# A small expert group in a routed mixture: its ring of weight halves, the weight conversion beside it, and who scales the next group's rows

## The chip, the cores and the metric

The kernel runs on one core of a Trainium2 chip. The metric is the device time of one execution in microseconds (us); lower is better. Times are given as the median of several executions, and the trace is of one further execution under the profiler.

## The reference

Three stages follow one another: attention with a sigmoid in place of the softmax, a top-1 mixture of 8 experts, and a dense feed-forward (FFN) over all 1792 tokens. All data are float32.

```python
attn = 1.0 / (1.0 + np.exp(-(scale * q @ k.T - np.log(S))))   # B=4, H=12, S=448, D=64
x = (attn @ v), rows of 768
...
logits = xn @ en.T / tau                # norms of rows and of expert_emb taken out
expert_idx = np.argmax(logits, axis=1)
gate_w = softmax(logits)[expert_idx]
for e in range(8):                      # w1[e] is 768 x 1024, w2[e] is 1024 x 768
    h = np.maximum(x[mask] @ w1[e], 0.0)
    out[mask] = gate_w[mask, None] * (h @ w2[e])
...
h = x @ w_in                            # 768 x 2048
return (h - np.tanh(h)) @ w_out         # 2048 x 768
```

## The kernel before, in words

Every float32 product is made of three products of rounded halves: high by high, low by high, high by low. A number is split by a cast on ScalarE (ACT), which gives the high half, and by a subtraction on VectorE (DVE), which gives the low one. TensorE (PE) runs the three products.

**Attention** takes 84 slots of scores, hand-ordered on PE (`manual_schedule`). Each slot costs ACT two sigmoids (L275, L276) and DVE one subtraction (L277, tile `al`) that the products with `v` wait for.

**Experts.** Tokens are sorted by expert into groups of 256 rows (`GR`). Two groups are planned early, then six more slots run (`run`, `NST` = 6). A group (`group`) has four column blocks of the first product (`NC1` = 4, tile `pth`, 36 matmuls a block, weights `w1raw`) and three of the second (`NC2` = 3, tile `pty`, 48 matmuls a block, weights `w2raw`). `split` makes the halves of 128 weight columns at a time into `ring`, which has four places (`NRING`), taken in turn by `turns[0]`; so a block uses one pair of places. After the first product of a group, `nxt` gathers the next group's rows by an indirect DMA on GpSimd (POOL), scales them by the gate (`gate_rows`, ACT, L807), transposes them on PE and splits them (`columns`: ACT L840, DVE L841, tiles `wi`, `xl`). A gathered group waits in `xg`; `wi0` holds the high half of its columns, so there is one such tile.

**The small slot.** One expert has a rest of at most 128 rows. It is done right after the first planned slot (`NFEW` = 1) by `prep_few` and `few`, with the operands exchanged: 128 rows stand still and 256 weight columns stream, 18 matmuls a block of the first product and 24 of the second. Weights are split by halves of the depth (`both(c, 0)` and `both(c, 1)`): block 0 goes to two tiles of its own (`few_h`, `few_l`), the others to pairs of the ring, listed in `s["parts"]`. Its results come out with rows standing and have to be turned (`turn`, two transposes through PSUM tile `xt`, of which there are two): `hidden` turns a block of the middle layer and splits it, `out` turns a block of the result. The PSUM tiles `xt` are shared with `columns`. Three chains (`A`, `V`, `T`, class `Line`) keep the small slot's own instructions on ACT, DVE and PE in the order in which they are written; all else is placed by a scheduler that works out times and priorities when the program is built. Each engine then runs its list in order.

**Conversion.** The FFN weights are split once into DRAM: 32 units (`conv_unit`), each with a load and a store on the queue of SyncE (SP) and seven instructions: ACT L1147 and L1158, DVE L1149, L1151, L1153, L1155, L1160 (tiles `ca`, `cr`). `NEARLY` units run in attention, `CPG` units are handed to each expert group until eight (`NFFN`) are left, and the last eight run in the FFN (`CPF`). In the experts they are put in at a low priority (`LATER`), behind the scaling of the next group's rows (`issue_after(self.xg_act.ins)`).

## Time and profile before

| what | us |
|---|---|
| median of 3 executions (1026.67 to 1028.25) | 1027.68 |
| the profiled execution, its own time | 1028.11 |
| its span, first to last instruction | 1026.4 |
| PE busy, share of the span | 993.7 (97%) |
| DVE busy | 786.8 (77%) |
| ACT busy | 554.3 (54%) |
| POOL busy | 218.5 (21%) |

Attention runs to about 223 us, the experts from there to about 544, the FFN from there to the end. In the profile a stretch is read by the number of PE instructions in it: matmuls of 256 columns follow each other about every 0.118 us when nothing is missing, so 8 us hold about 69 of them. A row's bracket, where there is one, gives the idle time ahead of it and what ended that.

### The profile page before, as it was taken

What the parts mean: (1) busy time and instruction counts of PE and PEld (TensorE: products, weight loads), DVE (VectorE), ACT (ScalarE), POOL (GpSimd) and SP (SyncE); (2) the same over time, 40 slices, a digit from 0 to 9 for tenths busy, and PEclk for the clock granted to TensorE, in tenths of its full rate; (3) what the DMA queues carried; (4) which work ended last, traced back from release to release, by engine and by line L of the source; (5) the groups of instructions that cost most, each with busy time, mean ns of one, the idle gap of its engine ahead of it and who ended that gap; (6) DMA issues with size and microseconds to landing.
All of it is one profiled execution on the core that took longest, in us unless ns stands there. A gap on an engine that the chain in (4) does not pass through costs nothing.

```text
span 1026.4 us, 16537 instructions
## 1 busy us (share of the span) xinstructions
PE 993.7 (97%) x6318; PEld 923.1 (90%) x6318; DVE 786.8 (77%) x1043; ACT 554.3 (54%) x698; POOL 218.5 (21%) x312
## 2 busy tenths in 40 slices
PE   8999999999998789999999999999999999999997
PEld 6877878789998789999999899999999999999997
DVE  6687777769977878989854888998897667766774
ACT  7788887876575767676643434344343332333230
POOL 8667667645800100100000000000001200000002
PEclk9999999999999989999999999999999999999999
DMA  6533434369568985965814555345524531233212
GB/s 174 138 89 116 119 85 123 113 213 369 208 216 278 358 294 191 332 218 193 270 64 152 193 175 185 144 170 185 197 111 154 200 112 65 102 123 118 98 62 108
DMA packets 83446, 174.87 MB, mean 170 GB/s; under 512 B 7623, under 2 KB 62942, under 8 KB 83358
## 3 DMA queue, kind: packets, MB, share of 16 engines
q1 hardware_dynamic: 79438, 155.56, 44.9%
q0 software_dynamic: 3760, 17.95, 4.9%
q8 instruction: 52, 0.85, 0.3%
q14 instruction: 36, 0.29, 0.1%
q10 hardware_dynamic: 160, 0.21, 0.1%
HBM read 156.28 MB, written 36.30 MB: 188 GB/s over the span
## 4 chain that ended last, share of the span: by engine, by line
issue 57%; PE 26%; ACT 6%; DVE 5%; POOL 3%; DMA 2%; SPq 0%; POOLq 0%; ACTq 0%; DVEq 0%
PE pth L902 8%; PE pty L902 7%; PE pav L291 5%; PE pq L268 4%; ACT ah L275 2%; ACT pq L276 2%; POOL out_dram L546 2%; PE pr L316 1%; DVE al L277 1%; DMA xg<-x_tok,gidx 1%; DMA kq<-in_k_dram 1%; ACT sq L333 1%; DVE ring L991 1%; PE xt L834 1%; PE pty L991 1%
## 5 line engine op out<-in xcount | busy, mean ns | idle before, releaser
L1306 PE MATMUL o<-wo,gh 128*128 128x384 f32 x896 | 240.4, 335 | 0.7 <-DVE acc L1319 0.7
L1255 PE MATMUL z<-yh,wi 128*128 128x512 f32 (+1 forms) x768 | 220.0, 365 | 0.4 <-PEq L1122 0.4
L1306 PEld LDWEIGHTS o<-wo,gh 128*128 128x128 f32 x896 | 163.0, 188 | 2.2 <-DVE acc L1319 1.0
L1255 PEld LDWEIGHTS z<-yh,wi 128*128 128x128 f32 x768 | 141.6, 188 | 15.7 <-issue 0.6
L1306 PE MATMUL o<-wo,gl 128*128 128x384 f32 x448 | 150.0, 335 | 0.5 <-DVE gl L1280 0.5
L902 PE MATMUL pth<-wi,ring 128*128 128x256 f32 x768 | 140.2, 282 | 1.2 <-DVE ring L893 0.6
L1255 PE MATMUL z<-yl,wi 128*128 128x384 f32 (+1 forms) x384 | 138.3, 364 | 0.0
L902 PE MATMUL pty<-hh,ring 128*128 128x256 f32 x736 | 136.9, 284 | 1.3 <-ACT ring L892 1.2
L546 POOL DMA_INDIRECT out_dram<-acc,toki x14 | 16.7, 1193 | 570.3 <-DVE acc L1319 569.1
L277 DVE TENSOR_TENSOR al<-pq,ah 128x896 fp32r<-128x896 f32 x84 | 91.3, 1088 | 43.5 <-ACT pq L276 43.3
L902 PEld LDWEIGHTS pth<-wi,ring 128*128 128x128 f32 x768 | 119.0, 189 | 2.4 <-DVE ring L893 0.8
L902 PEld LDWEIGHTS pty<-hh,ring 128*128 128x128 f32 x736 | 116.0, 191 | 1.8 <-ACT ring L892 1.5
L1319 DVE TENSOR_TENSOR acc<-o,acc 128x768 f32<-128x768 f32 x97 | 92.4, 953 | 31.8 <-PE o L1306 31.6
L902 PE MATMUL pth<-xl,ring 128*128 128x256 f32 x384 | 108.1, 282 | 0.0
L1279 ACT CAST gh<-r 128x896 fp32r<-128x896 f32 x32 | 30.1, 941 | 140.8 <-DVE r L1277 79.3
L902 PE MATMUL pty<-hl,ring 128*128 128x256 f32 x368 | 104.2, 284 | 0.3 <-DVE hl L920 0.3
L275 ACT ACTIVATE ah<-pq,bias_s 128x896 fp32r<-128x896 f32 x84 | 85.5, 1018 | 34.9 <-PE pq L268 34.2
L1263 ACT ACTIVATE t<-z 128x896 f32<-128x896 f32 x32 | 29.4, 920 | 107.2 <-PE z L1255 66.4
L1306 PEld LDWEIGHTS o<-wo,gl 128*128 128x128 f32 x448 | 84.1, 188 | 2.2 <-DVE gl L1280 0.8
L276 ACT ACTIVATE pq<-pq,bias_s 128x896 f32<-128x896 f32 x84 | 83.0, 988 | 0.0
L1255 PEld LDWEIGHTS z<-yl,wi 128*128 128x128 f32 x384 | 72.1, 188 | 7.4
L893 DVE TENSOR_TENSOR ring<-w1raw,ring 128x768 fp32r<-128x768 f32 x64 | 60.5, 953 | 23.5 <-ACT ring L892 23.2
(317 smaller groups left out, 1946.1 us busy)
## 6 DMA issues: line engine op xcount, KB each, us to landing
w1raw<-in_moe_w_dram SPq DMA_DIRECT2D x36, 768.0 KB
w2raw<-in_moe_w_dram SPq DMA_DIRECT2D x27, 1024.0 KB
wi<-dwi SPq DMA_DIRECT2D x32, 768.0 KB
wo<-dwo SPq DMA_DIRECT2D x32, 768.0 KB
cr<-in_moe_w_in_dram SPq DMA_DIRECT2D x16, 768.0 KB
dwi<-cr SPq DMA_DIRECT2D x16, 768.0 KB
cr<-in_moe_w_out_dram SPq DMA_DIRECT2D x16, 768.0 KB
dwo<-cr SPq DMA_DIRECT2D x16, 768.0 KB
```

What stands on the lines that cost most here:

```text
L268: nc.tensor.matmul(pq[:, x, :S], w[kt][p, c : c + P], w[qt][p, KW:], start=(m == 0), stop=(m == 2))
L275: nc.scalar.activation(hi, pv, AF.Sigmoid, **sc)
L276: self.last_sig = nc.scalar.activation(pv, pv, AF.Sigmoid, **sc)
L277: nc.vector.tensor_tensor(lo, pv, f32(hi), ALU.subtract)
L291: nc.tensor.matmul(pav[:, :S], vo(vv), aa[:, x], start=(b0 and m == 0), stop=(e and m == 2))
L546: i = self.nc.gpsimd.indirect_dma_start(**kw)
L893: self.last_split = nc.vector.tensor_tensor(wl, cols, f32(wh), ALU.subtract)
L902: self.last_mm = nc.tensor.matmul(pt[:, u], a[:, kk], b[:, kk], start=(n == 0), stop=(n == 3 * K - 1))
L1255: nc.tensor.matmul(z[:, G0[g] : G0[g] + GS[g]], wi[:, a, j * P : (j + 1) * P], yhl[half][g][b][:, j], start=(left[g] == 3 * NJ), stop=(lef ...
L1279: nc.scalar.copy(gv, r)
L1306: nc.tensor.matmul(o[:, w, :NW], a[:, u, i * P : (i + 1) * P], wo[:, b, w * NW : (w + 1) * NW], start=(n == 0), stop=(n == 3 * CH - 1),)
L1319: nc.vector.tensor_tensor(acc[i], ov, acc[i], ALU.add)
```

## The change

Six edits.

1. Conversion: `NEARLY` goes from 1 to 3 units in attention, and `CPG` from 6 for each group to the list 3, 4, 0, 4, 4, 3, 3, 0; the third entry is the group after which the small slot comes.
2. Ring: the first pair of the small slot is now the one after the pairs that the group's own second product takes (`NC2` = 3 further), so the order in which pairs are taken goes on without a pair being taken twice in a row.
3. Rows: behind the small slot's group the next rows are scaled by POOL (`pool=True`, `tensor_scalar`) instead of ACT. ACT's next `gate_rows` comes after the small slot's last ACT instruction (`issue_after(self.last_few)`).
4. PE: the small slot's matmuls come after the last matmul of its group (`T.last`).
5. Splits: the second half of a block's split is written after the turn of the block ahead (`hidden`), not together with the first half.
6. `nxt` is called one half block earlier.

```diff
-NEARLY, NFFN = 1, 8
+NEARLY, NFFN = 3, 8
-CPG, CPF = 6, 2
+CPG, CPF = (3, 4, 0, 4, 4, 3, 3, 0), 2
...
     def gate_rows(self, s, h):
-        self.xg_act = self.nc.scalar.activation(x[:, h, :DM], x[:, h, :DM], AF.Copy, scale=x[:, h, DM + 1 : DM + 2])
+        with self.tc.issue_after(self.last_few) if self.last_few is not None else ExitStack():
+            self.xg_act = self.nc.scalar.activation(x[:, h, :DM], x[:, h, :DM], AF.Copy, scale=x[:, h, DM + 1 : DM + 2])
...
+            if pool:
+                x = s["x"][:, h]
+                self.nc.gpsimd.tensor_scalar(x[:, : self.DM], x[:, : self.DM], x[:, self.DM + 1 : self.DM + 2], None, ALU.mult)
+            else:
+                self.gate_rows(s, h)
...
-                    for _ in range(CPG):
+                    for _ in range(conv.pop(0)):
...
-            k = turns[0] % NRING // 2
+            k = (turns[0] // 2 + NC2) % 2
...
         def few(s, nxt):
+            T.last = self.last_mm.ins
...
                     hidden(c - 1)
+                if c > 1:
+                    both(c + 1, 1)
                 product(c, pt, s["xt"], 1)
                 keep(c, pt, nc.scalar.activation, AF.Relu)
                 if c in (1, 2):
                     both(c + 2, 0)
-                    both(c + 2, 1)
...
                     both(NC1 + 1, 1)
+                    nxt()
...
                     both(NC1 + 2, 1)
-                    nxt()
             T.last = None
             out(NC2 - 1)
+            self.last_few = A.last
...
-                nxt = (lambda: prep(slots[i + 1], n)) if i + 1 < len(slots) else None
+                nxt = (lambda: prep(slots[i + 1], n, here)) if i + 1 < len(slots) else None
```

Three places show what this does to the lists of the engines.

PE where the first product of the small slot's group ends. `pth<-wi,ring` and `pty` of L902 (L908 in the new numbering) are the group's, all of L991 are the small slot's. Before:

```order
1359 L902 MATMUL pth<-wi_124,ring 128x256
1360 L991 MATMUL pth<-few_h,wi_124 128x256
1361 L962 MATMUL xt<-ident,xg 128x128 x2
1362 L964 MATMUL xt<-ident,xg 1x128
1363 L991 MATMUL pth<-few_h,wi_124 128x256
1364 L991 MATMUL pth<-few_l,wi_124 128x256
1365 L991 MATMUL pth<-few_h,wi_124 128x256 x2
...
1369 L902 MATMUL pty<-hh,ring 128x256
1370 L902 MATMUL pty<-hl,ring 128x256
```

After:

```order
1359 L908 MATMUL pth<-wi_124,ring 128x256
1360 L968 MATMUL xt<-ident,xg 128x128 x2
1361 L970 MATMUL xt<-ident,xg 1x128
1362 L908 MATMUL pty<-hh,ring 128x256
1363 L908 MATMUL pty<-hl,ring 128x256
1364 L908 MATMUL pty<-hh,ring 128x256
1365 L908 MATMUL pty<-hl,ring 128x256
```

Thirteen of the 18 matmuls of the small slot's first block stood between the group's two products; now they stand behind the group's last one.

ACT at the end of the group, with the first splits into the ring for the small slot (`ring<-w1raw_141`), before:

```order
304 L941 COPY yT_2705<-pty 128x2x256
305 L807 ACTIVATE xg<-xg 128x768 x2
306 L941 ISA
307 L941 COPY yT_2706<-pty 128x2x256
308 L991 CAST ring<-w1raw_141 128x3x2x128
309 L1147 ACTIVATE ca<-cr 128x768
310 L991 CAST ring<-w1raw_141 128x3x2x128
```

After:

```order
307 L947 COPY yT_2727<-pty 128x2x256
308 L997 CAST ring<-w1raw_141 128x3x2x128 x2
309 L947 ISA
310 L947 COPY yT_2728<-pty 128x2x256
311 L997 CAST ring<-w1raw_142 128x3x2x128 x2
```

The split of block 1 moved ahead of the group's second result, the scaling of rows (L807) and the conversion (L1147) left the place.

ACT at the start of the group that follows the small slot (`hh<-pth` is its first result block), after:

```order
339 L898 CAST ring<-w1raw_142 128x768
340 L997 ISA
341 L997 COPY yT_last<-xt 128x2x128
342 L809 ACTIVATE xg<-xg 128x768 x2
343 L1158 ACTIVATE ca<-cr 128x768 x2
344 L898 CAST ring<-w1raw_142 128x768
345 L925 ACTIVATE hh<-pth 128x512
```

Two scalings of rows and the first instructions of two units now stand ahead of `hh`; before, one scaling, one split and the end of a unit stood there:

```order
347 L991 COPY yT_last<-xt 128x2x128
348 L807 ACTIVATE xg<-xg 128x768
349 L892 CAST ring<-w1raw_142 128x768
350 L1158 CAST cr<-ca 128x768
351 L892 CAST ring<-w1raw_142 128x768
352 L919 ACTIVATE hh<-pth 128x512
```

What moved there is the second scaling, which came behind `hh`, and the units' first instructions.

## Rows read from the trace of the kernel before

**Rows 1.** Busy time by stretch: length, PE, PEld, DVE, ACT, POOL (instructions), clock, DMA.

```profile
224.00:312.00 88.00, 87.30 (x734) 86.51 (x735) 76.01 (x152) 58.12 (x84) 40.18 (x40) 1.00 0.81 276
312.00:384.00 72.00, 60.27 (x456) 56.72 (x455) 56.32 (x74) 49.27 (x73) 7.11 (x6) 0.93 0.89 310
384.00:544.00 160.00, 160.00 (x1348) 159.41 (x1347) 127.39 (x154) 100.01 (x132) 6.45 (x4) 1.00 0.61 203
...
360.00:368.00 8.00, 6.19 (x29) 5.70 (x30) 5.35 (x8) 2.74 (x5) 1.89 (x2) 0.51 1.03 381
```

**Rows 2.** Who waited for whom, PE, 312 to 384 us: total, times, longest.

```profile
PE xt L825 <- DVE xl L841: 2.6, 1, 2.6
PE xt L834 <- DVE xl L841: 2.0, 1, 2.0
```

**Rows 3.** Timeline of PE ahead of the second product: start, us, line, tiles, count.

```profile
314.47 0.28 PE L902 MATMUL pth<-wi,ring 128*128 128x256 f32 x1
315.55 0.39 PE L991 MATMUL pth<-few_h,wi 128*128 128x256 f32 x1 [0.81 <-ACT few_h L994]
...
319.08 0.28 PE L991 MATMUL pth<-few_h,wi 128*128 128x256 f32 x1
320.61 0.39 PE L902 MATMUL pty<-hh,ring 128*128 128x256 f32 x1 [1.25 <-ACT ring L892]
```

**Rows 4.** Timeline of PE in the small slot and behind it.

```profile
347.97 0.28 PE L991 MATMUL pty<-ring,hh 128*128 128x256 f32 x1
...
358.06 1.12 PE L834 MATMUL xt<-ident,xg 128*128 128x128 f32 x4 [2.02 <-DVE xl L841]
361.80 0.58 PE L825 MATMUL xt<-ident,xg 128*1 128x128 f32 x2 [2.62 <-DVE xl L841]
...
366.50 0.63 PE L991 MATMUL pty<-ring,hh 128*128 128x256 f32 x2
366.93 0.41 PE L991 MATMUL pty<-ring,hl 128*128 128x256 f32 x1
...
380.07 0.36 PE L902 MATMUL pth<-wi,ring 128*128 128x256 f32 x1 [0.30 <-DVE hl L920]
```

**Rows 5.** Groups by line, DVE, 337 to 364 us: count | busy, mean | idle.

```profile
L991 DVE TENSOR_TENSOR ring<-w2raw,ring 128x1024 fp32r<-128x1024 f32 x6 | 7.2, 1223 | 0.0
L991 DVE TENSOR_TENSOR ring<-w1raw,ring 128x768 fp32r<-128x768 f32 x6 | 5.6, 952 | 8.4 <-ACT ring L991 8.3
L1160 DVE TENSOR_TENSOR cr<-ca,cr 128x768 fp32r<-128x768 f32 x3 | 2.9, 954 | 0.0
...
L841 DVE TENSOR_TENSOR xl<-xt,wi 128x512 fp32r<-128x512 f32 x3 | 2.0, 686 | 0.0
...
L1149 DVE TENSOR_SCALAR ca<-ca 128x768 f32<-128x768 f32 x3 | 1.7, 553 | 0.0
```

**Rows 6.** Groups by line, ACT, 337 to 364 us.

```profile
L991 ACT CAST ring<-w1raw 128x768 fp32r<-128x768 f32 x6 | 4.7, 832 | 3.3 <-PE pty L902 3.3
L1147 ACT ACTIVATE ca<-cr 128x768 f32<-128x768 f32 x3 | 2.8, 919 | 0.6 <-DMA cr<-in_moe_w_in_dram 0.6
...
L807 ACT ACTIVATE xg<-xg 128x768 f32<-128x768 f32 x2 | 1.9, 934 | 0.0
```

**Rows 7.** Attention, 57 to 77 us: PE's waits, and one conversion step on DVE.

```profile
PE pq L268 <- DVE al L277: 0.9, 2, 0.5
...
59.94 1.25 DVE L1151 TENSOR_SCALAR ca<-ca 128x768 int32<-128x768 int32 x1
```

**Rows 8.** Groups by line, POOL, whole span: nearest operations to a scaling of rows.

```profile
L229 POOL TENSOR_TENSOR w2l<-kq,w2h 128x512 fp32r<-128x512 f32 x8 | 10.3, 1287 | 0.0
...
L464 POOL TENSOR_SCALAR lg<-u,itau 112x32 f32<-112x32 f32 x4 | 4.8, 1204 | 13.1 <-DVE u L326 13.1
```

**Rows 9.** An earlier rest of PE in attention, and the stretch behind it.

```profile
19.31 0.47 PE L268 MATMUL pq<-w2h 64*128 64x448 f32 x2 [1.32 <-DVE al L277]
...
20.00:22.00 2.00, 2.00 (x8) 1.47 (x5) 1.12 (x2) 2.00 (x3) 2.00 (x2) 0.50 0.75 229
```

More of the change, by code (lines that the diff above doesn't have):

```diff
@@ L765, in experts_early @@
     def experts_early(self, cx):
+        self.last_few = None
         self.pp = self.pool("plan", 1, cx)
@@ L806, in gate_rows, with gather_rows @@
         DM, x = self.DM, s["x"]
-        self.xg_act = self.nc.scalar.activation(x[:, h, :DM], x[:, h, :DM], AF.Copy, scale=x[:, h, DM + 1 : DM + 2])
-    def gather_rows(self, pl, slot):
+        with self.tc.issue_after(self.last_few) if self.last_few is not None else ExitStack():
+            self.xg_act = self.nc.scalar.activation(x[:, h, :DM], x[:, h, :DM], AF.Copy, scale=x[:, h, DM + 1 : DM + 2])
+    def gather_rows(self, pl, slot, pool=False):
         s = self.group_tiles(pl, slot)
@@ L813, in gather_rows @@
         for h in range(2):
-            self.gate_rows(s, h)
+            if pool:
[3 more added lines that the diff above has]
+                self.gate_rows(s, h)
         return s
@@ L946, in experts, with prep @@
         pst = lambda: ps.tile([P, 2, GR], F32, tag="x", name="xt")
-        def prep(slot, s):
-            s.update(self.gather_rows(pl, slot))
+        def prep(slot, s, pool=False):
+            s.update(self.gather_rows(pl, slot, pool))
             self.columns(s, pst)
@@ L1111, in second @@
             self.columns(self.s1, pst)
-        group(self.s0, self.e0, None, slice(0, GR), NWE, second, True, last_route)
+        conv = list(CPG)
+        group(self.s0, self.e0, None, slice(0, GR), NWE, second, conv, last_route)
         e, new = (self.reg(nc.sync, self.pl1[x], 0, n) for x, n in (("e", E - 1), ("new", 1)))
         oa = self.reg(nc.scalar, self.pl1["off"], 0, NT - 1)
-        group(self.s1, e, new, ds(oa, GR), 0, lambda: prep(0, s), True)
-        run(list(range(NST)), s, True, False)
+        group(self.s1, e, new, ds(oa, GR), 0, lambda: prep(0, s), conv)
+        run(list(range(NST)), s, conv, False)
         first = lambda: nc.sync.dma_start(f32(self.wi0).rearrange("p a b -> p (a b)"), self.win_s[0].rearrange("p a b -> p (a b)"))
         first()
+        self.last_few = None
         if NG > NST:
@@ L1126, in experts @@
                 prep(NST, s)
-                run(list(range(NST, NG)), s, False, True)
+                run(list(range(NST, NG)), s, None, True)
                 first()
```

## The prediction

> **What bounds the kernel now.** I read the busy times by stretch first. TensorE is busy through nearly all of the 1026.4 us, so the time falls only where PE stands still or runs slowly. From 384 to 544 us PE does 1348 matmuls in 160 us, 0.119 us each, with no gap; from 312 to 384 us it does 456 in 72 us [rows 1]. At 0.119 these are 54.3 us of work, so about 18 us are lost, in the small slot and its surroundings. The reader should see that this is the only large hole.
>
> The waits name three losses. First, ahead of the group's second product PE waits for the small slot's operands and then 1.25 us for a ring split, so the second product gets going at 320.61 [rows 3]. Second, in the small slot it waits 2.0 and 2.6 us for low halves of the next rows, both put down to DVE [rows 2, 4]. That engine holds 6 + 6 ring splits and three conversion units there [rows 5]: a unit is three steps of two operands at 0.954 and two of one at 0.553, 3.97 us, so three take 11.9 of 26.4 us in which DVE has no break. Third, the clock: behind those rests it is granted at 0.51 [rows 1], half of 2.4 GHz, and matmuls follow each other every 0.213 us (two and one more from 366.50 to 366.93, [rows 4]). A mean of 0.93 over 72 us is 0.07 x 72 / 0.5 = 10 us at 1.2 GHz, in which each us loses (0.213 - 0.119) / 0.213 = 0.44 us. Before 352 us there is no place for them, so the shorter rests of [rows 3] left the clock alone.
>
> **The change part by part.** Times of the replay are estimates from durations of before laid on the new order.
>
> *Filler moved.* Of the small slot's first block, 13 matmuls stood in the rest before the second product. They go behind it: 13 x 0.119 = +1.5 us there. The rest itself stays: its first products wait for ACT's splits of the group's own weights, which no edit moves, so 320.61 holds.
>
> *Second product and small slot.* The group's second product has 144 matmuls, 4 of them done; 140 more end at 337.2, the 18 of block 0 at 339.4. The ring in step lets the split of block 1 begin while the group's last product runs; with splits at 0.83 on ACT and 0.95 on DVE [rows 6, 5] they are then ready, and blocks 1 to 3 run at PE's pace: 54 x 0.119 = 6.4, to about 346 with the turns. In before PE began the second product of the small slot at 347.97 [rows 4]; so 1.5 late has become about 1.5 early. With 11.9 us of conversion gone, DVE waits for PE here and no longer PE for DVE.
>
> *Who is late next.* The last but one block. Its splits of `w2raw` can begin only when the turns are through, about 350; then DVE has four of these at 1.22, three low halves of the next rows at 0.69 and a short step, estimated at 0.4: 7.3 us [rows 5], of which the turn that ends the block's first half waits for all. So PE reaches the turn at about 357.3, where before it stood at 362.39 [rows 4], after a rest of some 3 us in an almost empty stretch of 4.5. Behind it stand 36 matmuls and the turns, 4.9 us at full clock: 362.2. In before the same ran at half clock to 369.4. Gain here: 5.0 + 2.2 = 7.2.
>
> *The group that follows.* PE is ready for its third block after two blocks of 36 and the transposes, 9.5 us later at 371.7; in before this block starts at 380.07, waiting for `hl` [rows 4]. But ACT now holds two scalings of rows (2 x 0.93) and two conversion starts (2 x 0.92) [rows 6] ahead of the first `hh`, behind a copy that waits for the small slot's last turn, which PE does 34 matmuls into this group, at 366. Copy to 366.5, scalings to 368.4, starts to 370.2, a split to 371.0, `hh` to 371.6; on DVE the units' one-operand steps and a split stand ahead of `hl`, which ends at 373.7. So PE waits 2.0 and the gain shrinks to 380.07 - 373.7 = 6.4. Two later waits of the same kind (conversion ahead of a low split and of a further `hl`), at one or half a DVE step of 0.95 each, cost 1.4. **Experts: -5.0**, bounds -7.2 (no queue late) and -3.5 (each twice as long). With 384 to 544 full, nothing behind it can give more back.
>
> *Clock.* With the filler gone, from 314.6 to 320.6 PE does three transposes and four matmuls, where it did 13 matmuls more [rows 3]. In attention a rest ending at 19.31 was followed by a granted clock of 0.50 [rows 9]; the rests of [rows 3] were not. Between none and eight us at half clock (0 to 3.6), I take **+1.5**. The rest before the turn at 357.3 is shorter than the 2.0 + 2.6 that made the clock fall in before: 0 to 2.3, I take **+0.8**.
>
> The Trainium skill, "TensorE: Matmul & The Clock Gate", section "What's actually happening", says that the throttled state is the default and activity releases it. By this a stretch that loses its filler would lose clock too, as [rows 9] shows and [rows 3] does not; by it alone the sum would be higher by the 2.1 us left open here.
>
> *Attention.* Two more units there. Where the one of before ran, PE waited 0.9 us for `al` [rows 7], with none in the neighbouring stretches. Two give **+1.8**; bounds 0 (they fall where DVE has room) and 3.0 (a step took 1.25 us there against 0.553 in the experts [rows 7, 5]).
>
> *Fewer units in other groups.* 21 in place of 23, but in stretches without waits: nothing. The small slot's group hands out none.
>
> *POOL.* The rows of the next group are needed at about 346, and gathered near 320. No scaling on POOL is in the trace. Its nearest rows are 1.20 us for 32 columns with a scalar for each partition and 1.29 for 512 columns of two operands [rows 8]; between 1.2 and 3.1 us each for 768, so two end by 330 at the latest. Zero; if a queue of POOL held them 15 us longer, it would count. ACT is relieved of 1.9 us in the rest, worth little, as PE waits there for splits ahead of it.
>
> A step of DVE took twice its usual time in attention beside POOL work [rows 7, 5]. The Trainium skill, "SBUF — State Buffer", section "SBUF: two separate sides", says that GpSimd and VectorE share a pair of ports that one instruction holds whole. By it DVE's low splits could stand behind each scaling, at most 2 x 3.1 us; the replay has over 3 us of room there, so it would leave up to 3 more.
>
> *Splits interleaved, `nxt` earlier.* Within the order replayed above.
>
> *Sum.* -5.0 + 1.5 + 0.8 + 1.8 = -0.9, on the profiled execution's 1028.11, which is 0.4 above the median of 1027.68. The forecast on the median is **1026.9**, -0.8. A difference of 0.2%, 2.06 us, is about what a measurement of this kernel can tell; the forecast lies within it.
>
> **The rivals.**
>
> *Faster: clock stays up.* The rests of [rows 3] did not cost clock and the new one is broken up by small work. Then both clock terms are zero: -5.0 + 1.8 = -3.2, about 1024.4; with the following group's queue on time -7.2 + 1.8 = -5.4, 1022.3. I put this case at 1023.4. For it: only one rest in 312 to 352 would be new. Against: the stretch 314.6 to 320.6 is nearly empty.
>
> *Slower: clock falls in both rests and stays down through dense work.* Place: from 320.61 on, the second product, and again from 357.3 on. Price 0.44 us per us. At the bounds, 3.6 + 2.3 against -5.0 + 1.8: +2.7, 1030.4. It decides from 3.2 us of clock loss on for any loss at all, and from 5.3 us, twelve us of dense work at 0.213, for over 0.2%. For it: in before 10 us went at half clock after one such rest [rows 1, 4]. Against: it needs both.
>
> *The change does not do what it says.* If the small slot's splits were early enough anyway, since its first block now starts a group later than the filler did, the ring step would move nothing, and conversion in the next groups takes back what it left: 1027.7.
>
> **How the numbers follow.** Forecast 0.40; faster rival 0.35; slower rival 0.19; no effect 0.06. The range reaches to both rivals, 1022.5 to 1030.6; the forecast's own is 1025.6 to 1029.7. Faster by over 0.2% 0.35, within 0.46, slower 0.19.
>
> **What would show it right or wrong.** In the trace of after: no conversion step on DVE from 337 to 362; no wait for low halves of rows of 2 us in the small slot; 456 matmuls of this stretch done before 384, and the third block of the next group starting near 373.7 in place of 380.07, plus what the clock took. The granted clock behind 320 and behind 357 tells the two clock terms apart: 1.00 in both is the faster rival, 0.5 for eight us behind 320 the slower. `hh` of the next group behind two scalings and two conversion starts, and waits of PE for it, show the queue term. The end of attention moving from 223 to about 225 shows the attention term. The prediction is wrong if the second product starts later than 320.61, if POOL's rows come after 346, or if a full stretch behind 384 gets gaps.

## The result

The changed kernel is slower. Its median is 1038.01 us (four runs, 1037.03 to 1041.91), against 1027.18 for the kernel before; the ratio is 1.0114, with a 95% interval of 1.0084 to 1.0145. That is 10.8 us more, outside the range of 1022.5 to 1030.6, and on the side to which the prediction gave 0.19. The profiled execution has a span of 1037.0 us, where that of before has 1026.4.

The first step is to cut the span at three places that can be read from the timeline of PE: the first matmul of the experts (`pth`), the last matmul of the small slot, and the first matmul of the FFN (`z`). The lengths between them, in us, worked out from the starts and ends of those rows:

| kernel | attention, to the first `pth` | from there to the small slot's end | from there to the FFN | FFN |
|---|---|---|---|---|
| before | 223.1 | 146.7 | 179.3 | 477.3 |
| after | 230.3 | 138.8 | 190.2 | 477.7 |
| difference | +7.2 | -7.9 | +10.9 | +0.4 |

So the stretch for which the change was written did become shorter, by about what was forecast. It was lost twice: ahead of it in attention and behind it in the groups that follow.

PE by stretch in the kernel after (length, then busy time and instructions of PE, PEld, DVE, ACT, POOL, then granted clock and DMA; a granted clock of 1.00 is 2.4 GHz, 0.50 is 1.2 GHz, and what lies between is a mix of the two). The row of 312 to 384 answers to that of [rows 1]; the row of 24 to 216 is attention without its two ends. The last row is that of the kernel before for attention:

```profile
24.00:216.00 192.00, 182.32 (x1072) 147.83 (x1071) 145.78 (x245) 156.00 (x195) 126.16 (x197) 0.99 0.42 129
312.00:384.00 72.00, 63.42 (x506) 61.15 (x505) 51.60 (x66) 45.95 (x69) 14.20 (x8) 0.95 0.80 264
408.00:424.00 16.00, 12.66 (x101) 11.84 (x100) 10.68 (x14) 10.01 (x14) 0.00 (x0) 1.00 0.52 173
448.00:464.00 16.00, 13.34 (x96) 12.73 (x95) 7.66 (x11) 7.78 (x11) 0.00 (x0) 0.89 0.54 193
...
24.00:216.00 192.00, 185.97 (x1106) 151.81 (x1104) 141.38 (x241) 158.03 (x197) 127.66 (x202) 1.00 0.40 119
```

In 312 to 384 us PE now does 506 instructions in place of 456, although everything there comes 7.2 us later. In exchange two stretches that were full before have holes: at 0.119 us each, 16 us hold some 135 matmuls, and here stand 101 and 96.

**Where attention loses.** Two places of the timeline, VectorE and then PE (start, length, engine, line, tiles; in brackets the idle time ahead and what ended it):

```profile
133.02 1.09 DVE L277 TENSOR_TENSOR al<-pq,ah 128x896 fp32r<-128x896 f32 x1 [1.00 <-ACT pq L276]
134.03 1.61 DVE L1160 TENSOR_SCALAR ca<-ca 128x768 f32<-128x768 f32 x1
135.67 0.70 DVE L1162 TENSOR_SCALAR ca<-ca 128x768 int32<-128x768 int32 x1
136.41 1.09 DVE L1164 SCALAR_TENSOR_TENSOR ca<-cr,ca 128x768 int32<-128x768 int32 x1
137.53 0.96 DVE L1166 SCALAR_TENSOR_TENSOR ca<-cr,ca 128x768 int32<-128x768 int32 x1
138.41 1.08 DVE L277 TENSOR_TENSOR al<-pq,ah 128x896 fp32r<-128x896 f32 x1
...
139.55 0.47 PE L268 MATMUL pq<-w2h 128*128 128x448 f32 x1 [2.65 <-DVE al L277]
...
140.60 0.57 PE L268 MATMUL pq<-w2h,w2l 128*128 128x448 f32 x1
```

Four steps of the third unit stand in a clump ahead of the subtraction `al` that PE needs: 4.4 us. PE rests for 2.65 us, and from about 140 us its matmuls are further apart; the granted clock of 136 to 144 us is 0.79. The second unit is cheaper. It shows as a step of 1.26 us on VectorE at 112.33, beside which POOL takes 3.11 us for a pair of products that take 2.40 elsewhere, and PE waits 1.39 us for POOL at 115.74.

**Where the groups behind lose.** POOL, ACT, DVE and PE around the first of the two holes; the last two rows are the gathers at these two places in the kernel before:

```profile
397.61 8.64 POOL L800 DMA_INDIRECT xg<-x_tok,gidx  x1 [0.30 <-issue]
...
411.60 0.93 ACT L809 ACTIVATE xg<-xg 128x768 f32<-128x768 f32 x1 [7.30 <-DMA xg<-x_tok,gidx]
412.44 0.81 ACT L898 CAST ring<-w1raw 128x768 fp32r<-128x768 f32 x1
...
413.28 0.96 DVE L899 TENSOR_TENSOR ring<-w1raw,ring 128x768 fp32r<-128x768 f32 x1 [7.26 <-ACT ring L898]
...
413.31 0.38 PE L908 MATMUL pth<-wi,ring 128*128 128x256 f32 x1 [1.51 <-ACT ring L898]
414.30 0.50 PE L908 MATMUL pth<-wi,ring 128*128 128x256 f32 x2 [0.49 <-DVE ring L899]
417.77 0.50 PE L908 MATMUL pth<-wi,ring 128*128 128x256 f32 x2 [1.07 <-DVE ring L899]
...
395.98 0.94 POOL L799 DMA_INDIRECT xg<-x_tok,gidx  x1 [0.30 <-issue]
430.96 3.61 POOL L799 DMA_INDIRECT xg<-x_tok,gidx  x1 [0.30 <-DVE ca L1153]
```

This is read from top to bottom. POOL needs 8.64 us to issue a gather that takes 0.94 in the kernel before. The rows land about 5 us later. ACT has come to the scaling of these rows and waits for them 7.30 us, since it does its list in order; the weight splits behind it start late, then VectorE's, then PE's matmuls. At 437 us the same happens again: 10.28 us of POOL, 7.28 of ACT, 1.98 of PE, and behind that the clock at 0.79.

The loss can be put to groups by counting their matmuls (144 of the second product in each). From the small slot's end, the five groups take 37.9, 35.5, 35.8, 36.3 and 33.4 us in the kernel before, and 40.0, 39.3, 41.6, 35.8 and 33.2 here. So 2.1 us are lost in the group next to the small slot, where PE waits for `hl`, and 3.8 and 5.8 in the two groups whose rows come late.

### The profile page after: what moved, and what is told of

Same layout as the page of the kernel before. It is cut to its first block, busy times and chain, and to the rows that moved or that the text cites. A ratio compares the mean times of both kernels' runs of the same rounds, so it can differ in the third digit from the quotient of the medians.

```text
span 1037.0 us, 16535 instructions
## 1 busy us (share of the span) xinstructions
PE 998.4 (96%) x6318; PEld 926.5 (89%) x6318; DVE 786.7 (76%) x1043; ACT 552.5 (53%) x696; POOL 235.8 (23%) x314
## 4 chain that ended last, share of the span: by engine, by line
issue 54%; DMA 2%; POOL 2%; PE 1%; ACT 0%; DVE 0%; POOLq 0%
DMA xg<-x_tok,gidx 2%; POOL out_dram L546 2%; PE pth L908 1%; PE pty L908 0%; ACT ring L898 0%; POOLq L1448 0%; ACT cr L1169 0%; POOL xg L800 0%; DVE hl L926 0%; DVE ring L899 0%; DVE cr L1171 0%; ACT wi L846 0%; ACT yT_last L947 0%; POOLq L546 0%; POOLq L1133 0%
## 5 line engine op out<-in xcount | busy, mean ns | idle before, releaser
L908 PE MATMUL pth<-wi,ring 128*128 128x256 f32 x768 | 142.9, 285 | 8.6 <-ACT ring L898 3.5
L908 PE MATMUL pty<-hh,ring 128*128 128x256 f32 x736 | 138.3, 286 | 3.6 <-ACT ring L898 3.6
L908 PEld LDWEIGHTS pth<-wi,ring 128*128 128x128 f32 x768 | 119.9, 190 | 11.0 <-ACT ring L898 4.1
L908 PEld LDWEIGHTS pty<-hh,ring 128*128 128x128 f32 x736 | 117.3, 194 | 4.3 <-ACT ring L898 4.2
L908 PE MATMUL pth<-xl,ring 128*128 128x256 f32 x384 | 108.6, 283 | 0.0
L908 PE MATMUL pty<-hl,ring 128*128 128x256 f32 x368 | 105.0, 286 | 0.0
```

The costliest lines, as they stand in the source:

```text
L908: self.last_mm = nc.tensor.matmul(pt[:, u], a[:, kk], b[:, kk], start=(n == 0), stop=(n == 3 * K - 1))
```

## The experiments

The theory after the result has two parts. **A:** the two added units cost attention the 7 us. **B:** the scaling that waits on ACT for a late gather costs the groups the 11 us; behind it stands **C**, that the gather is late because VectorE runs without a pause beside it. The rival to A is that any new placement costs that much; the rival to B is that VectorE is too full there in itself, or that the weights arrive late.

### One conversion unit in attention: e1_near1

```diff
-NEARLY, NFFN = 3, 8
-CPG, CPF = (3, 4, 0, 4, 4, 3, 3, 0), 2
+NEARLY, NFFN = 1, 8
+CPG, CPF = (3, 4, 0, 4, 4, 3, 3, 2), 2
```

> The changed kernel with one conversion unit in attention instead of three; the two others go to the last expert group, which has none. Theory A (the two units cost attention about 8.4 us: four conversion steps of 4.4 us on VectorE ahead of one subtraction al at 138.4 us, PE waits 2.65 us and its clock falls behind it): attention ends near 223 us again, the granted clock is 1.00 from 136 to 144, time 1038.0 - 8.4 = about 1029.6. Rival (the loss in attention is not the units' but comes with any new placement, as the routing steps on VectorE and GpSimd move too): attention still ends 5 us or more late, time above 1035.

Measured: 1025.82 us, ratio to before 0.9979 (0.9969 to 0.9990). It is 12.2 us faster than the changed kernel, more than expected. Attention ends at 223.7 us, 6.6 less, and there are 1109 instructions of PE from 24 to 216 us: A holds. The other half of the gain was not expected: from the small slot's end to the FFN it takes 183.2 us in place of 190.2, though the two groups still get four units each. The gathers show why. The first takes 1.26 us, the second 6.56, and ACT waits 3.9 us for rows in these groups, in place of 14.6. With attention 7 us shorter, the scheduler laid the steps on VectorE in another order, and the gather met another stretch of them. The amount of conversion does not tell the two apart: in the 73 us behind the small slot VectorE spends 30.6 us on it here and 27.7 in the changed kernel.

### The third unit alone: e9_after_near2

```diff
-NEARLY, NFFN = 3, 8
-CPG, CPF = (3, 4, 0, 4, 4, 3, 3, 0), 2
+NEARLY, NFFN = 2, 8
+CPG, CPF = (3, 4, 0, 4, 4, 3, 3, 1), 2
```

> The changed kernel with two conversion units in attention instead of three, the third in the last group. Theory A in detail (each unit's steps come in a clump of four on VectorE ahead of a subtraction; the second unit's clump at 98 to 104 us costs about 2 us, the third's at 134 to 138 costs about 4.5, its own 2.65 us rest and the clock behind it): the rest at 136 to 139 and the fall of the clock there are gone, 1038.0 - 4.5 = about 1033.5. Rival (a fixed price for each unit wherever it falls, 8.4 / 2 = 4.2 each, of which the second pays as much): the loss from 96 to 120 us is as large as the one removed; both rivals give about the same time, but the matmuls of PE by 120 us and by 150 us tell them apart: theory A has 13 to 20 fewer than the kernel before at 120 and no more at 150, the rival 25 fewer by 120.

Measured: 1028.96 us, ratio 1.0010 (0.9996 to 1.0024). From 24 to 216 us PE does 1099 instructions, against 1072 with three units, 1109 with one and 1115 with none (e12_e7_near0). At 192 / 1106 = 0.174 us each, the third unit costs 27 x 0.174 = 4.7 us, the second 1.7 and the first 1.0. Profiles with the same attention code differ by about 1 us of this: 1104 to 1110 instructions in the nine with one unit, 1072 to 1078 in the three with three units. So the third unit's price is shown, at 3.7 to 4.7 us, and the others' only roughly. The rest at 136 us and the fall of the clock are gone (1.00 granted). Counted from 24 us, it lacks 13 instructions of the kernel before by 120 us, 9 by 128 and 8 by 152, which is theory A's picture. The price is not the same for each unit; it hangs on where its clump of steps falls. Here too the groups gain beside that (182.4 us from the small slot's end to the FFN), with gathers of 1.24 and 6.55 us.

### Rows scaled by GpSimd in every group: e2_pool_all

```diff
-                self.nc.gpsimd.tensor_scalar(...)
+                self.xg_act = self.nc.gpsimd.tensor_scalar(...)
...
-                nxt = (lambda: prep(slots[i + 1], n, here)) ...
+                nxt = (lambda: prep(slots[i + 1], n, not first)) ...
```

> The changed kernel with the rows of every following group scaled by GpSimd, not only those behind the small slot's group. In the changed kernel ScalarE's scaling waits twice 7.3 us for the second gather, and the weight splits behind it in ScalarE's list come late. Theory B (that wait in ScalarE's order is what stops PE at 411 and 454): no weight split waits there, PE's waits of 1.5 and 2.0 us and the clock's fall are gone, though the gathers still take 8 to 10 us of GpSimd; time 1038.0 - 10 = about 1028. Rival (VectorE itself is too full there, or the weights arrive late): PE's waits stay, time above 1035. Second rival: the scaled rows come so late that the transposes in the second product wait for them, which PE then shows at another place, 1033 to 1040.

Measured: 1025.83 us, ratio 0.9985 (0.9972 to 0.9998), 12.2 us faster than the changed kernel. From the small slot's end to the FFN it takes 178.3 us, 11.9 less, and PE has no wait there up to the first matmul of the FFN. By group it is 3.1 us less in the first, where no scalings stand ahead of `hh` any more, 3.7 in the second and 5.8 in the third. Attention, whose code is the same, is 2.2 us shorter in this profile. A gather of 9.55 us is still in the trace, with scalings of 8.36 us for two behind it on POOL, and nobody waits for them; but it stands one group earlier. The first line of the edit hangs the conversion on GpSimd's scaling, its order is new, and the gathers of the two groups that lost are short here (1.28 to 1.66 us). So this run takes away ACT's wait and the late rows at once. The two are told apart by e8_e6_ring below: there the gathers of these same groups take 7.88 and 6.38 us, GpSimd scales, and the groups take 35.5 and 35.8 us, as in this run. B holds: it was ACT's place in the chain, not the lateness of the rows. That VectorE was too full there is excluded too, as it has more conversion behind the small slot here (29.9 us in 73) than in the changed kernel (27.7).

### No conversion in the two groups: e3_units_late

```diff
-CPG, CPF = (3, 4, 0, 4, 4, 3, 3, 0), 2
+CPG, CPF = (3, 4, 0, 0, 0, 5, 5, 4), 2
```

> The changed kernel with no conversion in the two groups behind the small slot; their eight units go to the three groups after these (5, 5 and 4). Theory C (a gather on GpSimd ends only when VectorE comes to a pause, and the conversion closes the pauses): the gathers of the two groups take 1 to 2 us instead of 8.6 and 10.3, ScalarE's scaling does not wait there, PE has no gap from 384 to 460; where conversion now is dense, later gathers take 5 us or more, and one or two losses of 5 us stand there instead: time 1028 to 1038. Rival (the gather is long because of its own data or queue at that place): the same two gathers stay at 8 to 10 us without conversion beside them.

Measured: 1036.26 us, ratio 1.0084 (1.0062 to 1.0106). The same gathers are short: 0.94 and 1.40 us in the first group, 1.00 and 1.70 in the second. ACT waits 2.0 us for rows in place of 14.6. That is for C and against a gather that is long by itself. My guess on where the units would then hurt was wrong: no gather is left by then, but the FFN waits for the last units. PE waits 4.9 us for `yh` ahead of the FFN's first matmul and later 2.4 for a load of `wi`, and from that first matmul on the FFN takes 482.8 us in place of 477.7. The five groups themselves are done in 179.5 us, against 189.8 in the changed kernel and 178.9 before.

### The kernel before with the list alone: e4_before_nosmall and e5_before_list

The first takes from the kernel before only what the small slot's group hands out, the second gives it the list of the changed kernel with one unit in attention.

```diff
-CPG, CPF = 6, 2
+CPG, CPF = (6, 6, 0, 6, 5, 0, 0, 0), 2     (first)
+CPG, CPF = (3, 4, 0, 4, 4, 3, 3, 2), 2     (second)
...
+                    for _ in range(conv.pop(0)):
```

> The kernel before with one edit alone: the small slot's group hands out no conversion (6, 6, 0, 6, 5 units by group instead of 6, 6, 6, 5). Theory D (the conversion on VectorE is what the small slot waited for, so most of the 7.8 us that the changed kernel gains there come from this edit): the rests of 2.0 and 2.6 us and the clock's fall behind them go, gain of 5 to 8 us in the small slot; if the two groups behind it then lose as in the changed kernel, 2 to 10 us are given back, as read from their gathers. Rival (the ring order or the interleaved splits make the gain): the small slot keeps its waits of 2 us and more, time within 2 us of before or above.

Measured: 1027.26 us, ratio 0.9998 (0.9986 to 1.0011). Theory D cannot be told by this run: three units still stand on VectorE from 337 to 364 us, the small slot keeps its rests of 2.0 and 3.1 us, and the clock falls to 0.57 granted from 360 to 368. What the small slot meets are units handed out by the groups ahead, which have not been done by then.

> The kernel before with the conversion list 3, 4, 0, 4, 4, 3, 3, 2 alone (one unit in attention as before, and none of the other edits). In the run with 6, 6, 0 the small slot still held three units on VectorE, left over from the groups ahead, and kept its waits; here only seven are handed out ahead of it. Theory D, mended (the units handed out earlier than the small slot, not its own entry, decide; without any unit there the small slot loses its rests): no conversion step on VectorE from 337 to 364, the waits of 2.0 and 2.6 us and the half clock behind them gone, small slot 5 to 8 us shorter; of this the two groups behind may give back 3 to 10 by long gathers. Rival (ring in step and interleaved splits are needed for it): a rest of 2 us or more and a fallen clock stay in the small slot.

Measured: 1027.87 us, ratio 0.9996 (0.9982 to 1.0010). Now less than half as much conversion stands on VectorE in that stretch (4.8 us by its rows, 11.9 before), and the small slot ends 5.3 us earlier (141.4 us behind the start of the experts, 146.7 before). So the list alone gives two thirds of the 7.9 us. The expectation holds only in part: the rest of 2.0 us is down to 0.3, but one of 2.2 us stays where 2.6 stood, and the clock still falls behind it, for a shorter time (0.66 granted from 358 to 360 us, 0.50 to 362). All of the gain is given back: 186.1 us from there to the FFN in place of 179.3, all in the first group (44.7 us in place of 37.9). The profiled execution took 1031.23 us, 3.4 above the median, so the loss is read from it with care. Here is the reason, POOL, ACT, VectorE and PE behind the small slot in this run:

```profile
361.81 12.62 POOL L799 DMA_INDIRECT xg<-x_tok,gidx  x1 [0.30 <-PE pty L991]
...
377.86 0.94 ACT L807 ACTIVATE xg<-xg 128x768 f32<-128x768 f32 x1 [5.65 <-DMA xg<-x_tok,gidx]
...
372.68 0.94 DVE L1154 SCALAR_TENSOR_TENSOR ca<-cr,ca 128x768 int32<-128x768 int32 x1
373.55 0.67 DVE L920 SCALAR_TENSOR_TENSOR hl<-pth,hh 128x512 fp32r<-128x512 f32 x1
...
379.57 0.58 PE L902 MATMUL pth<-wi,ring 128*128 128x256 f32 x1 [3.68 <-ACT ring L892]
```

The gather ends at 374.43, 0.88 us behind the start of the subtraction `hl`, which has an operand from PSUM (`pth`). From the gather's issue to it, 11.7 us, stand fifteen instructions of VectorE with all operands in SBUF, without a pause.

### Both repairs: e6_near1_pool_all

The edits of e1_near1 and e2_pool_all together.

> The changed kernel with both repairs: one conversion unit in attention (the other two to the last group) and the rows of every following group scaled by GpSimd. If the two losses are separate, as theory A and B have it, their repairs add up: 12.2 and 12.2 us taken off one after the other, less what the first alone already saved of the second (its ScalarE waits were 3.9 instead of 14.6 us): 1019 to 1021. Rival (both repairs act by the same thing, the place of the conversion units in the two groups): no better than either alone, 1025.

Measured: 1020.93 us, ratio 0.9928 (0.9909 to 0.9946): as expected, 17.1 us below the changed kernel. The two repairs overlap by 7.3 us, since the first alone had already shortened the gathers and with them this stage by 7.0 us. Attention ends at 224.7, the small slot takes 139.0, the groups behind it 178.1.

### The fourth edit undone: e7_e6_filler

```diff
-            T.last = self.last_mm.ins
```

> The run before with the fourth edit undone: the small slot's matmuls may again stand ahead of the group's second product. Theory E (the edit empties the rest of PE ahead of the second product, and the clock falls behind it: 27 matmuls too few from 312 to 328 in the first run of this study, and 0.79 granted in the changed kernel): the filler comes back, granted clock 1.00 there, 2 to 3.5 us faster than the run before. Rival (the small slot's block needs the splits of the group's place, and its early start only moves waits): within 1 us, or slower by the two splits that then stand ahead.

Measured: 1016.8 us, ratio 0.9897 (0.9880 to 0.9914), 4.1 us better than the run before it. PE by stretch ahead of the group's second product, in e6_near1_pool_all and then here:

```profile
312.00:320.00 8.00, 4.95 (x36) 4.15 (x34) 7.96 (x12) 6.88 (x11) 1.68 (x2) 0.89 0.63 246
320.00:328.00 8.00, 6.54 (x41) 6.54 (x42) 7.34 (x9) 3.40 (x4) 6.25 (x3) 0.68 0.83 244
...
312.00:320.00 8.00, 5.26 (x36) 4.22 (x36) 7.96 (x12) 7.57 (x12) 2.48 (x2) 1.00 0.58 212
320.00:328.00 8.00, 8.00 (x68) 8.00 (x69) 7.86 (x8) 3.33 (x4) 5.97 (x2) 1.00 0.83 252
```

The second product runs at full clock here. It does so in the kernel before and in e5_before_list as well; in e4_before_nosmall and in the three runs that follow, which keep the filler too, the clock falls at this place (0.70 to 0.77 granted from 320 to 328 us). So the filler does not hold the clock every time. The small slot's stage takes 139.0 us in e6_near1_pool_all, 137.1 to 137.8 in the three runs that keep the filler and lose the clock, and 135.3 here. That puts some 1.5 us on the filler, which is also what 13 matmuls take by count, and some 2 on the clock; it is one profile each, so the shares are an estimate.

### The second edit undone: e8_e6_ring

```diff
-            k = (turns[0] // 2 + NC2) % 2
+            k = turns[0] % NRING // 2
```

> The run with both repairs with the second edit undone: the small slot's first pair of the ring is again the one used last by its group. Theory F (the pair taken twice in a row makes the first split wait for the group's last product): ScalarE's split for block 1 waits again for PE's last pty, PE waits 0.7 us and more for the ring in blocks 1 and 2 of the small slot, and the parity seen by the following group moves too; 1 to 3 us slower. Rival (the first block of 18 matmuls now hides the split): within 0.7 us.

Measured: 1026.22 us, ratio 0.9986 (0.9974 to 0.9999), 5.3 us slower than e6_near1_pool_all. The size was more than expected and the place another. In the small slot's blocks 1 to 3 PE waits for no split at all, so the rival is right there. The small slot ends 2.0 us later, with a wait of 1.5 us for a copy that stands behind two splits on ACT. The other 4.7 us lie behind it: two conversion casts, another conversion start and two splits now stand ahead of the next group's `hh`, PE waits 2.4 us for `hl` at 375.83, and the clock falls (0.79 from 376 to 384 us); that group takes 41.6 us in place of 36.9. How much of that is the ring and how much the scheduler's new order for the conversion, this run does not tell.

The groups after it lose nothing, though two of their gathers are long. POOL, and then all engines by stretch (length, PE, PEld, DVE, ACT, POOL, clock, DMA):

```profile
393.69 7.88 POOL L800 DMA_INDIRECT xg<-x_tok,gidx  x1 [0.30 <-issue]
431.89 6.38 POOL L800 DMA_INDIRECT xg<-x_tok,gidx  x1 [0.30 <-issue]
...
400.00:416.00 16.00, 16.00 (x137) 16.00 (x137) 13.00 (x15) 9.51 (x13) 7.04 (x3) 1.00 0.96 318
432.00:448.00 16.00, 16.00 (x137) 16.00 (x136) 14.64 (x16) 9.17 (x13) 11.12 (x3) 1.00 0.93 315
```

These are the gathers behind which the changed kernel lost 3.8 and 5.8 us. With the scaling on GpSimd the rows are as late (the second half is scaled 47 and 85 us behind the small slot's end, against 43 and 86 in the changed kernel) and PE is full, which is what theory B says.

### Three more on the fastest: e10, e11, e12

Each starts from e7_e6_filler. The first writes both halves of a split together again, the second lets ACT scale the rows behind the small slot's group, the third has no unit in attention.

```diff
-                if c > 1:
-                    both(c + 1, 1)
...
+                    both(c + 2, 1)
```

> The fastest run so far (both repairs, fourth edit undone, 1016.8) with the fifth edit undone: both halves of a block's split are written together again. Theory G (the second half, written early, stands on ScalarE and VectorE ahead of the turned block's split, which PE needs first): PE waits about 0.5 to 1 us more for hh or hl in blocks 1 to 3 of the small slot, 0.5 to 2 us slower. Rival (with no conversion there both orders are early enough): within 0.5 us.

```diff
-prep(slots[i + 1], n, not first)
+prep(slots[i + 1], n, not first and not here)
```

> The fastest run so far with the rows behind the small slot's group scaled by ScalarE again (GpSimd keeps the others): two scalings of 0.93 us stand on ScalarE at about 328 us. Theory H (ScalarE has slack there, as PE waits for splits ahead of it): within 0.7 us of 1016.8. Rival (the two hold back the first splits into the ring for the small slot): PE waits up to 1.9 us more in blocks 1 and 2, 1 to 2 us slower.

```diff
-NEARLY, NFFN = 1, 8
-CPG, CPF = (3, 4, 0, 4, 4, 3, 3, 2), 2
+NEARLY, NFFN = 0, 8
+CPG, CPF = (3, 4, 0, 4, 4, 4, 4, 1), 2
```

> The fastest run so far with no conversion unit in attention at all; its unit goes to the last groups (list 3, 4, 0, 4, 4, 4, 4, 1). By theory A one unit costs attention 0.9 us of waits: attention 0.5 to 1.5 us shorter, 1015.3 to 1016.5. Rival (the groups pay as much as attention saves, or the first products of the FFN wait for a unit that comes late): 1016.8 or above.

Measured: 1018.19 (ratio 0.9896, 0.9871 to 0.9922), 1017.25 (0.9891, 0.9869 to 0.9913) and 1017.42 us (0.9888, 0.9863 to 0.9914). The intervals of all four lie over each other: the fifth edit, the third one at the small slot and the last unit of attention are each worth less than can be told here. The traces say a little more. In e10 PE waits for no `hh` or `hl` in the small slot's first product, so the wait that theory G names is not there; 0.6 us of wait are added later, at the next rows' transposes. In e11 no wait is added in blocks 1 and 2, which fits H. In e12 attention ends 0.5 us earlier, which is within what equal attention code differs by, and the time is not below 1016.8, as theory A had it. The clock ahead of the second product, which differs between the four profiles, hides what is left.

## Why the prediction was wrong

**The small slot: right in mechanism, better in size than the sum had it.** The conversion list gives 5.3 of the 7.9 us alone (e5_before_list); what gives the rest was not isolated. The rests of 2.0 and 2.6 us in [rows 2, 4] are gone, and from 336 to 372 us no conversion step stands on VectorE. PE in the profile after:

```profile
PE xt L997 <- DVE row L852: 1.2, 1, 1.2
PE xt L840 <- DVE xl L847: 0.3, 1, 0.3
PE pty L997 <- DVE ring L997: 0.2, 1, 0.2
...
363.96 0.41 PE L997 MATMUL xt<-ident,yT 128*128 128x128 f32 x2 [1.17 <-DVE row L852]
```

The turn forecast for 357.3 us, counted from an experts' start of 223.1, comes at 363.96 from a start of 230.3: 134.2 us behind the start forecast, 133.7 measured. That forecast has no clock term in it; with the two that the sum adds, the small slot's stage would be 4.9 us shorter than before, and it is 7.9. The second product starts 96.9 us behind the start of the experts, with 97.5 forecast. The reason that the forecast gave for the ring, though, has no run for it: with the old pairs the small slot's blocks did not wait either.

**The queue ahead of `hh`: right.** ACT has two scalings, two conversion starts and a split ahead of it; PE then waits 1.86 us for `hl`, with 2.0 forecast, and the third block of that group starts 150.1 us behind the start of the experts, with 150.6 forecast (without the clock) and 157.0 in the kernel before:

```profile
373.19 1.76 ACT L809 ACTIVATE xg<-xg 128x768 f32<-128x768 f32 x2
374.86 1.69 ACT L1158 ACTIVATE ca<-cr 128x768 f32<-128x768 f32 x2
376.45 0.82 ACT L898 CAST ring<-w1raw 128x768 fp32r<-128x768 f32 x1
377.17 0.59 ACT L925 ACTIVATE hh<-pth 128x512 fp32r<-128x512 f32 x1
...
380.35 0.36 PE L908 MATMUL pth<-wi,ring 128*128 128x256 f32 x1 [1.86 <-DVE hl L926]
```

**The clock in the two rests: right for the first, none for the second.** Behind the rest ahead of the second product the clock falls, in the kernel after to 0.79 in each of two stretches of 8 us, of which this is the second:

```profile
328.00:336.00 8.00, 8.00 (x57) 8.00 (x56) 5.56 (x7) 2.18 (x4) 5.97 (x2) 0.79 0.83 260
```

Of 69 matmuls that it could hold 57 are left, 1.4 us. Taken was 1.5. Behind the other rest, shorter than forecast (1.17 us), it stays at 1.00, so the 0.8 taken for it was not paid. The slower rival, which put its price on the clock in these two places, is not what happened.

**Attention: the first step that failed, by its size and by its bounds.** The step took the 0.9 us of waits beside the one unit in [rows 7] and counted it twice, with 3.0 us as the upper end. Measured are 34 instructions fewer from 24 to 216 us, 5.9 us, and 7.2 at the end of the stage; two further profiles with three units (e2_pool_all, e3_units_late) have 5.0 and 6.2 there. A unit's cost was taken as a price for each, but it depends on what its clump of steps delays. A clump of four steps is 3.0 us by the rows in the experts and 4.4 here; the next subtraction `al` can be late by all of it, and the clock then adds its own. The bound should have been the clump's length and a fallen clock behind it, for each unit.

**The groups behind: the larger step that failed.** The term for fewer units in other groups was "21 in place of 23, but in stretches without waits: nothing", and of the stage behind the small slot it says "With 384 to 544 full, nothing behind it can give more back." The prediction names a full stretch with gaps behind 384 as a sign that it is wrong, and that sign came. That VectorE was busy there for 127 of 160 us in [rows 1] was not read as a danger, since PE had no wait. Two things were missed. The list moves units but hardly their number in these two groups: in the 73 us behind the small slot seven conversion units end in the kernel before and six after, and VectorE spends 27.7 us on conversion in both. What changed is the order of the steps, which the scheduler laid anew: the gathers that took 0.94 and 3.61 us now meet rows of VectorE without a pause, of some 8 and 9 us. And the scaling on ACT stands in front of the weight splits, so that a late gather reaches PE through ACT's order. The prediction looked at who is late in the small slot and its next group, and not at the other consumers of a moved resource. Measured: +10.9 us, of which 2.2 were in the sum (7.2 gained at the small slot's end against 5.0 in all); these are the 2.1 us of the first group, and the 3.8 and 5.8 of the next two are the step that was put at nothing. Where their gathers' rows fall is the scheduler's doing, so the size of this loss is in part chance: the list with one unit in attention and two more in the last group (e1_near1) loses 7.0 us less here.

**The sum against the measured stages.** Small slot -4.9 in the sum (-7.2 and the two clock terms) and -7.9 measured, attention +1.8 and +7.2, groups +2.2 and +10.9, FFN 0 and +0.4. With attention at +1.8 and the groups at +2.2, the kernel would have been 3.5 us faster than before, about 1024.2, which is within the faster rival's 1022.3 to 1024.4, but not for its reason, as the clock did fall once. The change with both losses repaired, e6_near1_pool_all, is at 1020.9; it also takes the scalings away ahead of `hh`. Two small points of the working change nothing: eight us at half clock are 3.5 and not 3.6, and the 3.1 us taken as the upper bound of a scaling on GpSimd is not worked out from [rows 8] (measured are 5.97 us for two).

## What to carry to other kernels

When work is moved off a critical stretch, the place where it lands has to be replayed like the place that it leaves, on every engine, and so has every stretch whose order a scheduler lays anew, because an unbroken row of fillers can hold up a neighbour that is not in the diff at all. An instruction that waits for a DMA should not stand ahead of urgent work on an engine that runs in order: give it to an engine whose lateness nobody feels (here GpSimd, 9.5 us in the two groups). A full engine in a stretch where nobody waits is no proof of room.

## What the runs showed of the hardware

A gather on GpSimd (an indirect DMA that it issues) mostly does not end while VectorE runs one instruction behind the other with all operands in SBUF. In 14 of the 19 that took over 3 us it ended 0.82 to 0.90 us behind the first pause, or behind the start of the first instruction that has an operand in PSUM. In e7_e6_filler, POOL and then VectorE at the end of its row:

```profile
355.76 10.49 POOL L800 DMA_INDIRECT xg<-x_tok,gidx  x1 [0.30 <-issue]
...
363.62 0.94 DVE L1163 SCALAR_TENSOR_TENSOR ca<-cr,ca 128x768 int32<-128x768 int32 x1
364.49 0.94 DVE L899 TENSOR_TENSOR ring<-w1raw,ring 128x768 fp32r<-128x768 f32 x1
365.35 0.67 DVE L926 SCALAR_TENSOR_TENSOR hl<-pth,hh 128x512 fp32r<-128x512 f32 x1
```

VectorE has no pause from the gather's issue to 365.35; the gather ends at 366.25, 0.90 behind the start of `hl`. In the kernel after, the gather of 437.17 us ends at 447.45, 0.83 behind the pause of VectorE that begins at 446.62. The 19 gathers are those of the two kernels and the twelve runs; measured from the end of the last instruction of such a row, the 14 end 0.82 or 0.83 us later. The other five do not fit: three of 3.5 us end 1.66 us behind the end of a row, and two of 6.55 and 6.56 us end inside one. So the end of a row mostly decides, but is not always needed. That conversion on VectorE is the cause and not only goes along with it is shown by e3_units_late, where the same gathers are short without it.

The Trainium skill, "SBUF — State Buffer", section "SBUF: two separate sides", warns of this: a DMA that GpSimd issues needs descriptors which it writes itself, and it "cannot write the descriptors" while VectorE holds the pair of ports that the two have in common. The prediction drew on this section for the scaling behind the small slot's group, where the rule did no harm (two scalings in 5.97 us, PE waiting for neither), and did not carry it to the gathers. The rows agree with the warning and go beyond it. The section has VectorE's instructions in a two-port mode as the ones that keep descriptors from being written; one with two operands from SBUF holds the pair, by it, only against a GpSimd operation that reads SBUF. But from 361.95 to 365.35 us in e7_e6_filler VectorE runs only instructions that read two tensors (`ring`, `cr` and `ca`), and the gather, which takes 0.94 us elsewhere, does not end in these 3.4 us. Whether that is because the gather reads its list of rows (`gidx`) from SBUF, no run here shows.

A VectorE step beside POOL work can take longer, too: the first step of the third unit in attention took 1.61 us at 134.03, with POOL at work from 134.18 for 2.51 us on three subtractions, where it takes 0.55 in the experts. No run sets the two apart.
